# The rest of the third step with 64-column stationaries, a spectrum in two parts, and the two halves in another order

## The chip, the cores and the metric

The kernel runs on one core of a Trainium2 chip. The metric is the device time of one execution in microseconds: the median of three runs, and for the reading of stages one execution taken by the hardware profiler. The engines are named as in the profile: PE is the matrix engine (PEld its loading of stationary operands), DVE the vector engine, ACT the scalar engine, POOL GpSimd, SP the engine that here only issues transfers.

## The reference

A long convolution along 12480 positions for 128 channels, multiplied by its input, and then two feed-forward layers with a gate:

```python
h_filt = (np.maximum(pos_emb @ w1, 0.0) @ w2) * np.exp(-0.01 * pos)[:, None]
Uf = np.fft.rfft(x * v, n=2 * S, axis=1)
Hf = np.fft.rfft(h_filt, n=2 * S, axis=0)
x = x * np.fft.irfft(Uf * Hf[None], n=2 * S, axis=1)[:, :S, :]
h = x @ moe_w_in;  x = (h * np.clip(h + 3.0, 0.0, 6.0) / 6.0) @ moe_w_out
h = x @ moe2_w_in; x = np.where(h > 0.0, h, np.exp(np.minimum(h, 0.0)) - 1.0) @ moe2_w_out
```

S is 12480, the layers are 128 to 2048 to 128, all in float32.

## The kernel before

The transform has length 179 x 128 and is done as products with tables, in four steps, before the two layers.

**First step** (`first`, L352 to L367): 90 frequencies (NK) of each of 128 channels. `first_u` evacuates the signal on ACT into the spectrum `Au`, in two halves of 64 channels: half 0 in the tail of the big tile `qb`, half 1 in the tile `au`. An element of `Au` is (channel d, frequency k, real or imaginary r), 180 numbers to a channel.

**Second step** (`second`, L430): in octets of 8 frequencies, a product on PE (L425), two products on DVE with the filter's spectrum (L439), a sum on POOL back into `Au` (L444). The last of these are those of octet 11, halves 0 and 1.

**Third step** (`third`, L448 to L480): for each channel one product with the table `cs` over 128 partitions. The stationary operand is a slice of `Au`, the moving one 64 columns of `cs`. `third_main` takes the first 64 frequencies (KM) of one channel, real part into bank 0 and imaginary part into bank 1 of a two-bank tile `q`, each against two column sets of `cs` that go to the two halves of the output's partitions; a group has 8 channels. `third_rest` takes the last 32 frequencies (of which 26 are new, the other 6 are met by zeros in a later table), so its stationaries have 32 columns, and four products side by side fill the 128 partitions of the output. `third_out` copies the second bank to SBUF on ACT (L462) and writes difference and sum on DVE (L464) into `main` and `own`. The order is main of half 0, rest of halves 0 and 1, main of half 1. `own` is then copied with its partition halves exchanged into `other` by four transfers on SP (L525), 4 MB in all. Between the groups of main of half 1, SP issues the loads of `xT` (L533, into `au`, which that half frees) and of the third and fourth table `ti` (L507).

**Fourth step** (`fourth`, L541): 17 batches. In each, `ti` is the moving operand and `main`, `own`, `other` are the stationaries (L546), first the 128-partition products (`most`), then the 64-partition ones (`rest`), in turn the other way round. DVE multiplies the result into `xp`, which lies on `au` (L623, L626). Four tiles `ti` rotate (TB); a batch's table is loaded when the batch four before it is done. SP also loads the first pieces of the layers' weights.

**Weights:** the arrays of the layers arrive as 64-bit numbers and are turned into float32 by `weight_steps` (L214), 32 jobs of 256 columns: a load from the ACT or SP queue, two ACT operations (L230, L231), three DVE operations (L242 to L244), a POOL sum (L247) and a store (L225) from the ACT queue. Step k issues the load of job k+2, begins job k+1 on ACT and stores job k-1. The calls of `convert(rate)` are strewn over the second, third and fourth step; each adds its rate to a sum, and for each whole number one step is taken: 0.6, 0.3 and 0.9 for a call in the second, third and fourth step (RATE, L258). 34 steps and the last store are needed in all; `convert(1000)` behind the fourth step takes whatever is left.

**The two layers** (L615 on): units of 12 matrix products, PE-bound; all their loads of weights beyond three early pieces are issued on SP behind the fourth step.

All orders are written out by hand; each engine takes its instructions in program order. `bank` hands out PSUM: four two-bank tiles, tags px and py in turn, so that PE may be at most four groups ahead of DVE.

## Time and profile before

| what | us |
|---|---|
| median of three runs (lowest, highest) | 1391.97 (1388.36, 1392.3) |
| the profiled execution | 1385.58 |
| its span, first to last instruction | 1383.8 |
| third step in it, first to last product | 176.06 to 249.43 |
| fourth step, from there to the first product of the layers | 249.43 to 304.92 |

Times in the rows are counted from the span's start. A matrix product of float32 stands in the trace as two records of PE and two of PEld. In a list of groups, "busy, mean ns" is followed by the engine's idle time in front of them and what ended it; "issue" is time in which an engine waited for nothing that the profile shows. In the chain of waits each piece has its start, its length and what was done in it.

### The profile page before, as it was taken

Reading aid. Unit: us, or ns where it says so; the run is one execution under the profiler, and the core shown is the slowest. Engines: PE = TensorE matmul, PEld = TensorE weight load, DVE = VectorE, ACT = ScalarE, POOL = GpSimd, SP = SyncE. Lnnn points to the kernel's source line nnn. Section 1 sums busy time; section 2 is a strip of 40 time slices with the busy share of each in tenths; the row PEclk is TensorE's granted clock in tenths of the full one; section 3 lists DMA queues with packets and bytes.
Section 4 is the critical chain, followed back from the end, with each engine's and each line's share of the span. In section 5 each row is a group of like instructions: output and inputs, shape, how many; then the busy total and the mean of one; then the engine's idle time right before and its main releaser. Section 6 shows DMA issues by size and latency. Waiting matters only on the chain.

```text
span 1383.8 us, 23826 instructions
## 1 busy us (share of the span) xinstructions
PE 1339.5 (97%) x9696; PEld 1140.3 (82%) x9696; DVE 1133.9 (82%) x1196; ACT 987.9 (71%) x1163; POOL 390.9 (28%) x278
## 2 busy tenths in 40 slices
PE   9999976599999999999999999999999999999998
PEld 9999976487788888888888888888888888888898
DVE  6737764379998888888888888888888888889897
ACT  5655522139887778877878777877787777787876
POOL 1026620031522223223222222322322222222223
PEclk9999999799999999999999999999999999999999
DMA  8913225971000000000000000000000000000000
GB/s 271 273 57 115 75 71 130 324 236 59 0 8 8 1 8 8 8 8 1 8 8 8 8 1 9 8 8 8 1 8 9 8 0 9 8 9 8 9 1 19
DMA packets 32093, 62.90 MB, mean 45 GB/s; under 512 B 3786, under 2 KB 9200, under 8 KB 31728
## 3 DMA queue, kind: packets, MB, share of 16 engines
q1 hardware_dynamic: 24640, 52.40, 12.4%
q10 hardware_dynamic: 7344, 8.98, 2.0%
q8 instruction: 76, 1.25, 0.4%
q14 instruction: 33, 0.27, 0.1%
HBM read 46.59 MB, written 10.58 MB: 41 GB/s over the span
## 4 chain that ended last, share of the span: by engine, by line
PE 90%; issue 3%; DVE 3%; DMA 2%; ACT 1%; POOL 0%; SPq 0%; ACTq 0%; DVEq 0%; POOLq 0%
PE o L746 36%; PE h L702 36%; PE pa L356 4%; PE q L453 4%; PE z L425 3%; PE y L546 2%; PE h L415 1%; PE r L406 1%; PE pr L310 1%; DVE gs L736 1%; DMA w<-w_scratch 1%; DMA ti<-in_ti 1%; DVE g L723 1%; DMA cv<-in_mw 0%; DMA au<-in_xT 0%
## 5 line engine op out<-in xcount | busy, mean ns | idle before, releaser
L746 PE MATMUL o<-gs,w 128*128 128x512 f32 (+1 forms) x2400 | 570.8, 386 | 0.4 <-DVE gs L736 0.3
L746 PEld LDWEIGHTS o<-gs,w 128*128 128x128 f32 x2400 | 445.0, 188 | 92.3 <-DVE gs L736 0.8
L715 POOL TENSOR_SCALAR a<-a 128x1024 f32<-128x1024 f32 (+1 forms) x200 | 292.0, 1460 | 725.9 <-ACT a L714 721.5
L736 DVE TENSOR_TENSOR gs<-g,gs 128x1024 fp32r<-128x1024 f32 (+1 forms) x400 | 483.7, 1210 | 4.5 <-ACT gs L731 3.7
L731 ACT CAST gs<-g 128x1024 fp32r<-128x1024 f32 (+1 forms) x400 | 409.8, 1024 | 55.2 <-DVE g L723 53.6
L723 DVE SCALAR_TENSOR_TENSOR g<-a,h 128x1024 f32<-128x1024 f32 (+1 forms) x200 | 238.7, 1194 | 123.3 <-ACT a L712 123.2
L702 PE MATMUL h<-xs,w 128*128 128x512 f32 (+1 forms) x1200 | 302.9, 388 | 0.4 <-DVE g L723 0.4
L702 PE MATMUL h<-x,w 128*128 128x512 f32 (+1 forms) x1200 | 297.9, 384 | 0.2 <-ACT a L714 0.2
L714 ACT ACTIVATE a<-h 128x1024 f32<-128x1024 f32 (+1 forms) x200 | 201.3, 1006 | 93.8 <-PE h L702 92.6
L702 PEld LDWEIGHTS h<-xs,w 128*128 128x128 f32 x1200 | 223.0, 188 | 49.2 <-DVE g L723 1.4
L702 PEld LDWEIGHTS h<-x,w 128*128 128x128 f32 x1200 | 223.1, 188 | 43.8 <-issue 0.5
L712 ACT ACTIVATE a<-h,bounds 128x1024 f32<-128x1024 f32 (+1 forms) x200 | 219.1, 1096 | 52.6 <-PE h L702 52.4
L725 DVE SCALAR_TENSOR_TENSOR g<-a,h 128x1024 f32<-128x1024 f32 (+1 forms) x200 | 237.4, 1187 | 0.2 <-POOL a L715 0.2
L247 POOL TENSOR_TENSOR cv<-cv 128x256 int32<-128x256 int32 x32 | 23.4, 732 | 127.8 <-DVE cv L244 127.8
L546 PE MATMUL y<-ti,qb 128*64 128x97 f32 (+3 forms) x1040 | 41.0, 261 | 14.5 <-DMA ti<-in_ti 11.5
L546 PEld LDWEIGHTS y<-ti,qb 128*64 128x64 f32 (+1 forms) x1040 | 37.5, 145 | 17.9 <-issue 7.6
L230 ACT ACTIVATE cv<-cv 128x256 f32<-128x256 f32 x32 | 14.3, 448 | 47.9 <-POOL cv L247 28.1
L444 POOL TENSOR_TENSOR qb<-qb,bp 128x1024 f32<-128x1024 f32 (+1 forms) x12 | 26.9, 2242 | 73.4 <-PE h L415 71.1
L356 PE MATMUL pa<-tab,cv 98*64 98x180 f32 x512 | 44.0, 316 | 0.0
L453 PE MATMUL q<-cs,au 128*32 128x64 f32 (+1 forms) x1024 | 27.7, 234 | 14.2 <-issue 14.2
L464 DVE TENSOR_TENSOR qb<-q,au 128x512 f32<-128x512 f32 (+2 forms) x34 | 20.7, 647 | 25.1 <-ACT au L462 22.2
L356 PEld LDWEIGHTS pa<-tab,cv 98*64 98x64 f32 x512 | 37.7, 137 | 3.3
(68 smaller groups left out, 806.8 us busy)
## 6 DMA issues: line engine op xcount, KB each, us to landing
uv<-in_xc SPq DMA_DIRECT2D x32, 196.0 KB
out_T<-y SPq DMA_DIRECT2D x23, 256.0 KB
au<-in_xT SPq DMA_DIRECT2D x8, 720.0 KB
qb<-in_gm SPq DMA_DIRECT2D x22, 256.0 KB
ti<-in_ti SPq DMA_DIRECT2D x16, 294.0 KB
cv<-in_mw ACTq DMA_DIRECT2D x18, 256.0 KB
uv<-in_vc SPq DMA_DIRECT2D x22, 196.0 KB
w_scratch<-cv ACTq DMA_DIRECT2D x32, 128.0 KB
```

What stands on the lines that cost most here:

```text
L356: nc.tensor.matmul(pa[f * HN:(f + 1) * HN, j, :2 * NK], lhsT=src(j, f), rhs=table[:, f], start=True, stop=True)
L453: nc.tensor.matmul(q[p:p + width, r, j * HN:(j + 1) * HN], lhsT=stationary(j, p, r), rhs=csr[:, r, p // width % 2], start=True, stop=True,)
L546: nc.tensor.matmul(y[c * HD:(c + 1) * HD, b, off:off + w], lhsT=lhsT, rhs=rhs[:, H1 - w:], start=(b, c) in fresh, stop=done, skip_group_ch ...
L702: nc.tensor.matmul(h[:, j], lhsT=wslice(2 * m - 2, a, 2 * u + j), rhs=x[:, b], start=i == 0, stop=i == 2)
L712: nc.scalar.activation(a, h, AF.Relu, bias=three)
L714: nc.scalar.activation(a, h, AF.Exp)
L715: nc.gpsimd.tensor_scalar(a, a, 1.0, 0.0, op0=ALU.min, op1=ALU.max)
L723: nc.vector.scalar_tensor_tensor(g, a, 6.0, h, op0=ALU.min, op1=ALU.mult)
L725: nc.vector.scalar_tensor_tensor(g, a, -1.0, h, op0=ALU.add, op1=ALU.max)
L731: nc.scalar.copy(t[:, 0], g)
L736: nc.vector.tensor_tensor(out=t[:, 1], in0=g, in1=t[:, 0].bitcast(F32), op=ALU.subtract)
L746: nc.tensor.matmul(o[:, :WID[t]], lhsT=wslice(2 * m - 1, a, 2 * u + j), rhs=gs[:, b, j], start=u == 0 and j == 0 and i == 0, stop=u == NU ...
```

## The change

The spectrum is split: `AuM` holds the first 64 frequencies of each channel (130 numbers to a channel, two of them padding), `AuR` the other 26 (54 numbers to a channel, two of them zero). `first_u` evacuates with two ACT operations in the place of one.

The rest of the third step takes real and imaginary part of a channel's 26 frequencies as one stationary of 52 columns (64 are read, the other 12 are neighbours whose results nobody uses). One product goes against a new column set, `csx`, of 68 columns; another takes a copy with real and imaginary part exchanged, made by ACT (`turned`, two operations for a group of 7 channels of both halves) in two small tiles that POOL clears first. The two halves of the channels fill the two halves of the output. ACT copies the second bank as before; DVE combines with four operations (`scalar_tensor_tensor`, the sign from a column) into `own` and `stage`. `stage`, not `own`, is the source of the exchange, and a transfer moves 52 partitions of 8704 bytes.

The order is: main of half 1, its first 32 channels; the rest of both halves in ten groups; the exchange; main of half 1, the other 32 channels; main of half 0. `main` of half 0 lies on `stage` and on `AuR` of half 0. `xT` comes in 13 pieces: four issued between the groups of the rest, nine between the groups of main of half 0. Six tiles `ti` rotate, four of them in the place of `AuM` of half 0. The rates are 0.55, 0.25 and 0.75. `fourth` does the 64-partition products first in the even batches; they now have 52 partitions. The order of the channels is the natural one, so two host permutations go.

```diff
-KM, KR = 64, 32
+KM, KR = 64, NK - 64
+KW = 2 * KR
+NG = len(BATCHES)
...
+    MS, RS = 2 * (KM + 1), 2 * (KR + 1)
+    AM, AR = HD * MS, HD * RS
+    SL = 2 * NG * HD * 2
+    MQ = N2 * HD
+    MAIN1, STAGE = 2 * SL, 2 * SL + MQ
+    AR0 = STAGE + SL
+    AM0 = max(AR0 + AR + GUARD, STAGE + MQ)
...
-    RATE = (0.6, 0.3, 0.9)
+    RATE = (0.55, 0.25, 0.75)
...
-        nc.scalar.mul(to, pa[:, :, :2 * NK].rearrange(form, r=2), scale)
+        for z, a, b in to:
+            nc.scalar.mul(z, pa[:, :, 2 * a:2 * b].rearrange(form, r=2), scale)
...
+    def turned(e0, n):
+        sw = sws[e0 // ET % 2]
+        for hf in range(2):
+            nc.scalar.copy(
+                sw[:, hf * ET * KW:(hf * ET + n) * KW].rearrange("p (e k r) -> p e k r", e=n, r=2), AuR[hf][:, e0:e0 + n, :, ::-1]
+            )
+
+    def third_rest(e0, n):
+        sw = sws[e0 // ET % 2]
+        q = bank("q", [128, 2, 4 * N2])
+        for j in range(n):
+            for r in range(2):
+                for hf in range(2):
+                    z, at = (sw, (hf * ET + j) * KW) if r else (ends[hf], (e0 + j) * RS)
+                    nc.tensor.matmul(
+                        q[hf * HD:(hf + 1) * HD, r, j * EW:(j + 1) * EW], lhsT=z[:, at:at + HD], rhs=csx[:, r, hf],
+                        start=True, stop=True,
+                    )
+        qs = half(q, n * EW)
+        for x, to in enumerate((own, stage)):
+            first, second = (
+                z.rearrange("p (e x m) -> p x m e", e=n, x=2)[:, x] for z in (q[:, 0, :n * EW], qs)
+            )
+            for o, (a, b) in enumerate(((second, first), (first, second))):
+                nc.vector.scalar_tensor_tensor(
+                    to[:, o, :, e0:e0 + n], a, column[:, 2 - o:3 - o], b, op0=ALU.mult, op1=ALU.add,
+                )
...
+    ET = 7
+    TB, TW = 6, max(BLOCKS) * H1
...
+    xcuts = [*range(0, AW, XP), AW, S]
...
+    for sw in sws:
+        nc.gpsimd.memset(sw, 0.0)
+    turned(*rests[0])
+    for s0 in range(0, HD // 2, 8):
+        third_main(1, s0, 8)
         convert(RATE[1])
-    for hf in range(2):
-        for out in [third_rest(hf, e0, n) for e0, n in groups([8] * 4)]:
-            out()
-            convert(RATE[1])
-    for a, b in ((0, 8), (8, HN // 2)):
+    for i, (e0, n) in enumerate(rests):
+        if i + 1 < len(rests):
+            turned(*rests[i + 1])
+        third_rest(e0, n)
+        if i in (1, 3, 5, 7):
+            load_x()
+        convert(RATE[1])
+    for o in range(2):
         for p in range(2):
             nc.sync.dma_start(
-                other[p * HD:(p + 1) * HD, :, a:b].rearrange("p o g h e t -> p o (g h e t)"),
-                own[(1 - p) * HD:(2 - p) * HD, :, a:b].rearrange("p o g h e t -> p o (g h e t)"),
+                other[p * HD:p * HD + KW, o].rearrange("p m e -> p (m e)"),
+                stage[(1 - p) * HD:(1 - p) * HD + KW, o].rearrange("p m e -> p (m e)"),
             )
-    for s0, n in groups([8] * 7 + [4, 2, 2]):
-        third_main(1, s0, n)
-        if (s0 + n) % EX == 0:
-            a, b = xload.pop(0)
-            nc.sync.dma_start(xp[:, a:b], xT[:, a:b])
-        if s0 in (16, 32):
-            load_ti(s0 // 16 + 1)
+    for s0 in range(HD // 2, HD, 8):
+        third_main(1, s0, 8)
+        convert(RATE[1])
+    for s0, n in groups([8] * 7 + [4, 4]):
+        third_main(0, s0, n)
+        load_x()
+        if s0 in (32, 40):
+            load_ti(s0 // 8 - 2)
         convert(RATE[1] if s0 < 56 else 0)
+    for i in range(4, TB):
+        load_ti(i)
...
-        for k, part in enumerate((most, rest) if i % 2 == 0 else (rest, most)):
+        for k, part in enumerate((rest, most) if i % 2 == 0 else (most, rest)):
```

## Rows read from the trace of the kernel before

**Rows 1.** The page, part 1: busy time and instructions of each engine

```profile
PE 1339.5 (97%) x9696; PEld 1140.3 (82%) x9696; DVE 1133.9 (82%) x1196; ACT 987.9 (71%) x1163; POOL 390.9 (28%) x278
```

**Rows 2.** Busy by stretch: length, PE, PEld, DVE, ACT, POOL, PEclk, DMA, GB/s

```profile
0.00:80.00 80.00, 78.87 (x921) 73.33 (x922) 52.98 (x127) 47.65 (x109) 5.56 (x10) 1.00 0.81 243
...
176.06:193.77 17.71, 17.71 (x513) 17.64 (x513) 12.25 (x25) 6.27 (x13) 5.84 (x7) 0.87 0.33 102
193.77:224.27 30.50, 17.71 (x1070) 16.19 (x1068) 14.08 (x25) 7.28 (x15) 1.61 (x3) 1.00 0.12 35
224.27:249.43 25.16, 17.78 (x469) 17.57 (x469) 11.90 (x24) 6.03 (x13) 1.46 (x2) 0.80 0.98 222
249.43:304.92 55.49, 40.95 (x1049) 37.50 (x1045) 31.02 (x64) 12.04 (x30) 12.52 (x16) 0.88 0.86 291
...
276.00:296.00 20.00, 20.00 (x598) 18.74 (x596) 15.64 (x31) 4.71 (x12) 5.14 (x7) 0.99 0.77 223
```

**Rows 3.** The chain of waits from 80 to 345 us, in order of time

```profile
195.04 1.99 PE q L453 x128
197.03 1.89 issue
...
224.27 7.87 PE q L453 x251
232.14 1.99 issue
234.13 5.51 PE q L453 x124
239.65 5.39 issue
...
250.11 6.44 DMA cv<-in_mw
...
263.46 9.81 DMA ti<-in_ti
...
298.97 1.65 issue
```

**Rows 4.** Transfers of the whole run: a queue's packets, MB, share; issues, KB each

```profile
q8 instruction: 76, 1.25, 0.4%
...
ti<-in_ti SPq DMA_DIRECT2D x16, 294.0 KB
cv<-in_mw ACTq DMA_DIRECT2D x18, 256.0 KB
...
w_scratch<-cv ACTq DMA_DIRECT2D x32, 128.0 KB
...
qb<-qb SPq DMA_DIRECT2D x2, 1536.0 KB
...
qb<-qb SPq DMA_DIRECT2D x2, 512.0 KB
```

**Rows 5.** Groups by line and shape, 176 to 250 us

```profile
L462 ACT COPY au<-q 128x512 f32<-128x512 f32 x15 | 8.8, 587 | 36.0 <-PE q L453 32.6 <-DVE qb L464 3.4
...
L464 DVE TENSOR_TENSOR qb<-q,au 128x256 f32<-128x256 f32 x2 | 0.7, 414 | 0.0
```

**Rows 6.** Instructions in order of time, 158 to 200 us

```profile
179.78 0.59 ACT L462 COPY tab<-q 128x512 f32<-128x512 f32 x1 [2.85 <-PE q L453]
...
181.30 0.73 POOL L444 TENSOR_TENSOR au<-qb,bp 128x256 f32<-128x256 f32 x1
```

**Rows 7.** Instructions in order of time at the end of the fourth step

```profile
301.13 0.45 ACT L230 ACTIVATE cv<-cv 128x256 f32<-128x256 f32 x1 [1.71 <-DMA cv<-in_mw]
...
301.87 0.42 DVE L242 SCALAR_TENSOR_TENSOR cv<-cv,bounds 128x256 f32<-128x256 f32 x1
...
304.92 5.37 PEld L702 LDWEIGHTS h<-xs,w 128*128 128x128 f32 x24
...
305.55 0.62 ACT L662 CAST xs<-au 128x512 fp32r<-128x512 f32 x1 [0.90 <-POOL cv L247]
...
306.63 1.12 ACT L712 ACTIVATE a<-h,bounds 128x1024 f32<-128x1024 f32 x1 [0.45 <-PE h L702]
```

More of the change, by code (lines that the diff above doesn't have):

```diff
@@ L81, in tables @@
     cs = np.concatenate([c[:, :HN], end, inner, c[:, :1], inner, -end, -c[:, 1:HN]], axis=1)
+    passes = (c, np.concatenate([c[:, :1], inner, -end], axis=1))
+    sets = np.full((2, NG, 2), -1)
+    for g, banks in enumerate(BATCHES):
+        for b, ms in enumerate(banks):
+            sets[b, g, :len(ms)] = ms
+    extra = [
+        np.where(order.ravel() < 0, 0.0, z[:, order.ravel()]) for z in passes for order in (sets, sets[::-1])
+    ]
+    cs = np.concatenate([cs, *extra], axis=1)
     ends = (m == 0) | (m == HN)
@@ L87, in tables, with entries @@
     none = np.zeros_like(t[0, 0])
-    def entries(ms):
+    def entries(ms, place):
         pairs = []
         for m in ms:
-            if m == 0:
-                pairs += [(t[0, 0], none), (t[0, 1], none)]
-            elif m == HN:
-                pairs += [(none, t[m, 0]), (none, t[m, 1])]
+            if m in (0, HN):
+                pairs += [(t[m, i], none)[::1 - 2 * (place and m == HN)] for i in range(2)]
             else:
@@ L165, in tile_kernel, with parts, spectrum @@
     lds = lctx.enter_context(tc.tile_pool(name="lds", bufs=1))
-    uv = lds.tile([H1, 10 * VT], F32, name="uv")
-    Au = [z.rearrange("p (d k r) -> p d k r", r=2, k=NK) for z in (qb[:, 2 * QW - AW:], au[:, :AW])]
+    uv = lds.tile([H1, 8 * VT], F32, name="uv")
+    def parts(z, at, n, w):
+        return z[:, at:at + n].rearrange("p (d k r) -> p d k r", k=w + 1, r=2)[:, :, :w]
+    AuM = [parts(qb, AM0, AM, KM), parts(au, 0, AM, KM)]
+    AuR = [parts(qb, AR0, AR, KR), parts(au, AM, AR, KR)]
+    ends = [qb[:, AR0:AR0 + AR + GUARD], au[:, AM:AW]]
+    for z in ends:
+        nc.gpsimd.memset(z[:, :AR].rearrange("p (d x) -> p d x", x=RS)[:, :, KW:], 0.0)
+        nc.gpsimd.memset(z[:, AR:], 0.0)
+    def spectrum(hf, k0, n):
+        return (AuM[hf][:, :, k0:k0 + n] if k0 < KM else AuR[hf][:, :, k0 - KM:k0 - KM + n])
     Ar = qb[:, :RW].rearrange("p (x f) -> p x f", f=FO)
     Rk = qb[:, :RW].rearrange("p (k c) -> p k c", k=NK)
-    main = qb[:, :QW].rearrange("p (o g c h e t) -> p o g c h e t", o=2, c=2, h=2, e=KR, t=2)
-    own, other = (
-        qb[:, QW + i * N2 * HD:QW + (i + 1) * N2 * HD].rearrange("p (o g h e t) -> p o g h e t", o=2, h=2, e=KR, t=2)
-        for i in range(2)
+    main = [
+        qb[:, z:z + MQ].rearrange("p (o g e t) -> p o g e t", o=2, e=HD, t=2) for z in (STAGE, MAIN1)
+    ]
+    own, other, stage = (
+        qb[:, z:z + SL].rearrange("p (o m e) -> p o m e", o=2, e=HD) for z in (0, SL, STAGE)
     )
@@ L177, in tile_kernel @@
         z[:H1, i * VT:(i + 1) * VT].rearrange("p (d f i) -> p d f i", f=2, i=HN)
-        for z in (uv, cv) for i in range(z.shape[1] // VT)
+        for z in (uv, cv, qb[:, RW + RF + D:RW + RF + D + 2 * VT]) for i in range(z.shape[1] // VT)
     ]
@@ L181, in tile_kernel @@
     xts, vts, uts = uvs[:DEEP], uvs[DEEP:2 * DEEP], uvs[2 * DEEP:]
-    rest = qb[:, RW:2 * QW - AW]
+    rest = qb[:, RW:AR0]
     GN = 8
@@ L468, in third_out, with half @@
             )
-    def third_main(hf, s0, n):
-        third(
-            hf, n, lambda j, p, r: Au[hf][:, s0 + j, :KM, r], HD,
-            lambda o: main[:, o, :, s0 // KR, hf, s0 % KR:s0 % KR + n],
-        )()
-    def third_rest(hf, e0, n):
-        return third(
-            hf, n, lambda j, p, r: Au[hf][:, p // HD * KR + e0 + j, NK - KR:, r], KR,
-            lambda o: own[:, o, :, hf, e0:e0 + n],
-        )
+    def half(q, n):
+        qs = qss[thirds[0] % len(qss)][:, :n]
+        thirds[0] += 1
+        nc.scalar.copy(qs, q[:, 1, :n])
+        return qs
@@ L554, in fourth @@
             off, k, found = 0, 0, []
-            for m in ms:
+            for t, m in enumerate(ms):
                 for sg in (1, 0):
```

113 lines of the change are left out of this document (59 added, 54 removed).

## The prediction

> **What bounds the kernel now.** Start with the page's first part [rows 1]: PE is busy for 97% of the span. That is an average over a long, full stage (the two layers, from 304.92 us on) and the steps before it, which aren't full; so look next at busy time by stretch [rows 2]. The third step takes 73.4 us (17.71 + 30.50 + 25.16), the fourth 55.5 us with PE busy for only 40.95. Nothing in the change touches the steady work of the layers. What can be won lies in these 128.9 us, and PE's own pace says how much.
>
> The chain of waits gives that pace. Main runs at 7.87 us for 251 records, 31.4 ns each [rows 3]; main's 512 records of a half need 16.1 us. The fourth step runs at 598 records in 20 us, 33.4 ns each [rows 2], so its 1040 records need 34.8 us. Both halves' main and the fourth step are therefore 67 us, and the rest has 1024 records in 30.5 us less the 46 records of main that fall into that stretch (1.4 us): 29.1 us.
>
> Three losses show. First, in the rest PE does 128 records in 1.99 us and then stands still for 1.89 us with nothing that it waits for ("issue") [rows 3]; the last such pauses are 1.6 us. These pauses don't fall on the ends of groups: 46 records of the rest precede the first one, then 128 between each two. The instruction queue moved 1.25 MB in 76 packets, 16.4 KB each [rows 4]; PE and PEld have 19392 instructions [rows 1], 64 bytes each if nearly all of these bytes are theirs, so a packet holds 128 products with their loads. I read the pauses as PE waiting for its next packet, one each 3.6 to 3.9 us. Main uses a packet in 128 x 31.4 ns = 4.0 us and just escapes. Second, while the copies run (DMA share 0.98, 222 GB/s), the pauses come to main too, 1.99 and 5.39 us [rows 3]: 515 records take 1.4 + 25.16 = 26.6 us where 16.1 would do, 10.5 us lost. Third, the fourth step waits for tables `ti`, which SP queues behind the copies and `xT` (9.81 us in the chain) [rows 3]: 55.5 us against 34.8.
>
> **The change part by part.** *First and second step.* ACT evacuates each of 32 tiles with two operations in the place of one, under 0.6 us more on an engine that is busy for 47.65 of 80 us; PE has 78.87 [rows 2]. Hidden; uncovered it would be at most some 6 us (32 x 0.2, the fixed part of an operation). One weight step fewer is taken in the second step: between nothing and three DVE operations of 0.42 us [rows 7]; taken at nothing.
>
> *Main of half 1, first part:* 256 records at the opening pace of 17.71 us for 513 [rows 2]: 8.8 us. Behind it a wait is added: ACT's `turned` stands ahead of the first evacuation and needs POOL's last sum, at 181.30 + 0.73 = 182.0 [rows 6], and the clearing of its tile (744 numbers on POOL, at most 3 x 0.73 us by the 256-wide sum, at least the fixed tenths of a microsecond; near 1). With two copies of 364 numbers at less than 0.59 us [rows 5], the first evacuation starts near 184.2 and not at 179.78 [rows 6]. Queued behind it are ACT's evacuations, then DVE's sums, then PE from the fifth group on; PE's four tiles cover it until about 185 us, so the delay itself costs PE little, but ACT and DVE begin the rest four groups behind.
>
> *Rest:* 1024 records become 512, of 68 columns: 31.4 x 68/64 = 33.4 ns, 17.1 us, and a packet then lasts 4.3 us, longer than 3.9, so the pauses go. What is late next is DVE: four operations of 238 numbers, at most 0.414 each by the 256-wide row [rows 5], with a quarter of a weight step 1.9 us for a group, 17.8 us for 9.14 groups, and 4 groups of arrears. ACT has 0.56 + 2 x 0.5 + 0.2 = 1.8 us. Bounds for PE's part 17.1 and 24 (all arrears paid); I take 19, nearer to the floor since PE may run four groups ahead. Gain: 10.
>
> *Exchange:* 4 x 52 rows of 8704 bytes are 1.81 MB, against 4 MB (two of 1536 and two of 512 KB [rows 4]): 0.43 of the loss of 10.5, 4.5 us. At 222 GB/s the copies take 8.2 us. DVE's writes of main of half 0 wait for their end (`stage` lies under them); PE has eight groups' work between, so this is covered up to some 12 us. A rule of the Trainium skill, "DMA: Bandwidth & Descriptors", section "Why a DMA increments its semaphore by 16 and not by 1", speaks against the new shape: the number of DMA engines that share a transfer is the largest up to 16 that divides the slowest dimension, so 52 rows get 13 where 64 got 16. By it the copies would take 10.1 us (an estimate) and the sum would be about 1 us more; no row here shows a transfer of 52 rows.
>
> *Rest of main:* 768 records at 31.4 ns, 24.1 us, plus those 4.5 and what nine pieces of `xT` (4.3 MB, 14.6 us at 291 GB/s [rows 2]) do to the packets: nothing, as between 276 and 296 us, where DMA share is 0.77 and PE never stops [rows 2], or the same loss per microsecond as the copies, 6.1. I take 2.5, nearer to the first row, since `xT` comes like the tables from memory.
>
> The third step's sum: 8.8 + 19 + 24.1 + 4.5 + 2.5 = 58.9 us against 73.4, so 14.5 less; it ends at 235.
>
> *Fourth step:* four tables are there or on the way before main ends, two more queue right behind, and `xT` is ahead of its use. Demand: 13 tables of 294 KB, 12.75 weight steps of 256 + 128 KB [rows 4] and 0.8 MB of weights, 9.5 MB, 33 us at 291 GB/s. So PE's 34.8 us bind, plus one pause of 1.65 [rows 3]: 36.4, which is 19.1 less. Other order, 52 instead of 64 rows: the same 1040 records.
>
> *Start of the layers:* the rates give 13.2 + 6.25 + 12.75 = 32.2 steps where 34 are needed (before: 36.6). Steps 33 and 34 and the last store now stand between the fourth step and the layers, in the queues of DVE, ACT and POOL. The last load is issued near the fourth step's end and lands some 3 us later; ACT 0.9, DVE 1.2, POOL 0.7, and ACT's store waits for that. ACT's first evacuation of the layers came 1.7 us after PE's start, behind just such a wait for POOL [rows 7]; now about 5.5. PE has three tiles and stops: plus 3.8 us, bounds 1 (the load was early) and 6.5 (a load of 6.44 [rows 3]).
>
> Sum: -14.5 - 19.1 + 3.8 = -29.8 us; on the profiled execution's 1385.58 that is 1355.8. Its own time is 6.4 below the median of the three runs, and the forecast is made for a median: 1362.
>
> **The rivals.** *The pauses stay.* If PE stands still for a cause that goes with the array's work and not with packets, the rest gains nothing: before, 512 products in fours are 128 turns of 64 columns, now 256 in pairs are 128 turns of 68; 29.1 x 68/64 = 31 us, 12 more: 1374. Against it: the pauses keep step with 128 records and not with groups, and main, with the same tiles, has none. The Trainium skill, "Runtime: NRT & Kernel Launch", section "Instruction fetch mechanics", says that fetching is hidden behind the engine's issue; by that rule the cause would be another and this rival's 1374 holds; the trace, with 1.89 us for each 16.4 KB, speaks against the rule. Chance 0.12.
>
> *Transfers stay the bound.* From the first copy to the fourth step's end the kernel moved 25.16 x 222 + 55.49 x 291 = 21.7 MB; 2.4 of it goes, 2.1 of `xT` come earlier: 17.2 MB from 208 us on. At 291 GB/s that ends at 267, under my 271; at 230, as while the copies ran, at 283: 1374. For it: shares of 0.98 and 0.86 [rows 2]; against: much of the fourth step's share fell while PE waited for queue order. Chance 0.15.
>
> *No stalls at all:* neither `xT` nor the last steps cost anything, and DVE keeps up: 1352. Chance 0.17.
>
> *Slower: DVE's scattered writes.* The four operations write runs of 7 numbers 256 bytes apart and read PSUM at a stride of 68. If that broke their pace, the rest would take as long as DVE needs. The other gains are 10 us less than the sum, so it decides above 19 + 30 = 49 us for the rest, 1.25 us an operation, three times the 256-wide row; at 1.5 us, 58 us, 1401. For it: no row has this pattern; against: the sums of before write scattered too and have 414 ns [rows 5]. Chance 0.05.
>
> **How the numbers follow.** Forecast 0.51, rivals 0.12, 0.15, 0.17, 0.05. Terms at their ends: rest -1.9 / +5, `xT` -2.5 / +3.6, layers -2.8 / +2.7, fourth step -1.6 / +4; not all fall one way, so the likeliest case has 1353 to 1374, which also takes in three rivals' centres; their own spread makes it 1348 to 1379, and what lies outside is the slow case and the two rivals together. A difference of 0.3% (4 us) is about what a measurement of this kernel can tell from no change. Faster by more: 0.92; same: 0.03 (both rivals and a dear start); slower: 0.05.
>
> **What would show it.** Right: 512 records of the rest in 17 to 21 us without pauses; third step ending near 235, fourth near 271 without waits for `ti`; the first evacuation of the layers 4 to 6 us behind PE's start. Wrong: pauses of 1.6 us or more per 128 records; operations of the rest above 0.5 us; PE waiting for DVE throughout the rest; waits for `ti` or for a load of weights in the fourth step.

## The result and the profile after

The changed kernel has a median of 1355.3 us (four runs, 1353.46 to 1356.6) against 1390.16 us of the kernel before in the same set: a ratio of 0.9754, 95% interval 0.972 to 0.9788. The profiled execution took 1354.19 us, its span 1352.4 us against 1383.8.

Four stages, cut at the first product of the third step, the first of the fourth and the first of the layers, show where the 31.4 us of the span went (us; all kernels of this document, each from its profiled execution; ratios are against the kernel before, run beside it):

| kernel | third step begins | third | fourth | layers | median | ratio, 95% interval |
|---|---|---|---|---|---|---|
| before | 176.1 | 73.4 | 55.4 | 1078.9 | 1390.16 | |
| after | 169.8 | 66.4 | 39.1 | 1077.1 | 1355.3 | 0.9754 (0.972 to 0.9788) |
| a1_rates | 171.8 | 67.1 | 39.8 | 1069.9 | 1349.74 | 0.9722 (0.9705 to 0.974) |
| a2_order | 170.1 | 62.2 | 41.5 | 1077.1 | 1352.37 | 0.9734 (0.9713 to 0.9755) |
| a3_rows64 | 170.4 | 65.6 | 40.3 | 1077.6 | 1356.27 | 0.9768 (0.975 to 0.9786) |
| b1_pad | 169.9 | 72.9 | 57.3 | 1078.9 | 1381.6 | 0.9951 (0.9934 to 0.9968) |
| b3_shift | 175.8 | 74.0 | 56.6 | 1069.8 | 1378.91 | 0.9938 (0.9918 to 0.9958) |
| a5_imm | 169.9 | 65.5 | 40.5 | 1078.0 | 1352.73 | 0.9748 (0.9732 to 0.9764) |
| a4_noexchange | 170.4 | 62.7 | 39.0 | 1078.2 | 1351.8 | 0.9738 (0.9722 to 0.9754) |
| b2_groups4 | 175.5 | 80.6 | 57.3 | 1078.8 | 1394.07 (one run) | |
| a6_pairs | 170.9 | 58.3 | 39.9 | 1078.3 | 1351.12 | 0.9731 (0.9707 to 0.9755) |
| a7_pairs_rates | 171.3 | 63.7 | 41.2 | 1069.9 | 1348.45 | 0.9704 (0.9673 to 0.9736) |
| a8_cover | 170.9 | 61.8 | 39.6 | 1069.9 | 1343.12 | 0.9675 (0.9652 to 0.9699) |
| a9_xlate | 170.7 | 66.2 | 43.2 | 1078.3 | 1358.27 | 0.9777 (0.9749 to 0.9805) |

The kernel before had medians of 1387.84 to 1388.3 us in the sets of the other kernels and 1390.16 in that of the kernel after, so a difference of two medians from different sets can be some 2 us off; the ratios are free of that.

So before to after is -6.3 (the third step begins earlier), -7.0, -16.3 and -1.8. The forecast had 0, -14.5, -19.1 and +3.8. The sum is nearly the forecast's -29.8, but not one of its four parts is: that is what the rest of this text is about.

The page's first part for the kernel after, which answers to [rows 1]: 512 records of PE fewer (256 products), and PE's share is one point higher.

```profile
PE 1321.7 (98%) x9184; PEld 1135.0 (84%) x9184; DVE 1144.7 (85%) x1218; ACT 996.2 (74%) x1216; POOL 397.1 (29%) x284
```

Busy time by stretch of the kernel after (the columns are those of [rows 2]): main of half 1's first part; the rest; the rest of main; the fourth step; the start of the layers.

```profile
169.78:179.89 10.11, 10.11 (x263) 10.11 (x265) 3.98 (x9) 3.12 (x7) 5.79 (x7) 0.76 0.67 209
179.89:201.00 21.11, 17.72 (x512) 17.11 (x508) 18.85 (x36) 13.83 (x34) 1.47 (x2) 0.92 0.33 97
201.00:236.20 35.20, 25.59 (x779) 24.49 (x775) 24.77 (x51) 9.47 (x21) 2.94 (x4) 1.00 0.70 222
236.20:275.31 39.11, 36.99 (x1040) 34.04 (x1040) 29.17 (x56) 11.74 (x29) 11.52 (x14) 1.00 0.80 247
275.31:300.00 24.69, 17.54 (x69) 13.73 (x68) 20.40 (x29) 16.82 (x22) 4.50 (x6) 0.86 0.59 181
```

The rest's 512 records keep PE busy for 17.7 us and take 21.1. The 768 records of main behind it (11 neighbours count with them) keep it busy for 25.6 us and take 35.2: most of what the third step still loses lies here. The fourth step has 2.1 us without work where before it had 14.5 [rows 2].

The chain of waits of the kernel after, second and third step, in the columns of [rows 3] (L463 is the second step's product, L491 main's, L523 the rest's, L533 the rest's combination on DVE, L497 main's, L598 the exchange):

```profile
93.59 1.94 PE z L463 x16
...
179.89 1.28 PE q L523 x42
181.17 0.73 issue
181.90 4.00 PE q L523 x126
185.90 2.58 issue
188.48 3.43 PE q L523 x55
...
196.02 9.07 DVE qb L533 x16
...
206.22 2.92 DVE qb L533 x8
209.14 2.36 DVE qb L497 x4
...
212.17 0.41 SPq L598
212.58 0.05 issue
212.63 10.82 DMA qb<-qb
```

Two pauses of PE, 0.73 and 2.58 us, are left in the rest. Behind the second the clock falls: from 188.48 to 191.70 us the granted clock is 0.50, the lower of its two levels (1.2 GHz), and 57 records take 3.22 us, where at full clock 126 took 4.00. Then the chain goes over to DVE, which works off the rest until 209.14, eight microseconds after PE has left it, and then to the exchange. The waits of PE from 201.00 to 236.30 us of the same kernel (in total, times, longest) price each of these for the rest of main:

```profile
PE q L491 <- issue: 5.2, 3, 2.7
PE q L491 <- DVE qb L533: 3.0, 2, 1.8
PE q L491 <- DVE qb L497: 1.1, 1, 1.1
```

5.2 us are pauses, 3.0 DVE's arrears, and 1.1 the exchange, for which DVE waits before it writes `main` of half 0.

The groups of DVE in the third step of the kernel after, which answer to [rows 5]:

```profile
L533 DVE SCALAR_TENSOR_TENSOR qb<-au,column,q 128x238 f32<-128x238 f32 x12 | 7.9, 659 | 2.1 <-ACT au L506 2.1
...
L497 DVE TENSOR_TENSOR qb<-q,tab 128x512 f32<-128x512 f32 x12 | 7.7, 685 | 13.5 <-DMA qb<-qb 8.6 <-ACT tab L506 5.0
```

238 numbers take as long as main's 512.

Instructions in order of time where the fourth step of the kernel after ends and the layers begin, which answers to [rows 7] (L266 to L283 belong to a weight step, L777 is the layers' product, L787 its first evacuation):

```profile
275.31 1.65 PE L777 MATMUL h<-xs,w 128*128 128x512 f32 x6
...
281.26 0.43 ACT L266 ACTIVATE cv<-cv 128x256 f32<-128x256 f32 x1 [3.03 <-POOL cv L283]
...
283.08 0.72 POOL L283 TENSOR_TENSOR cv<-cv 128x256 int32<-128x256 int32 x1 [2.14 <-DVE cv L280]
...
284.72 2.11 ACT L787 ACTIVATE a<-h,bounds 128x1024 f32<-128x1024 f32 x2
...
287.14 4.69 PE L777 MATMUL h<-xs,w 128*128 128x512 f32 x12 [6.41 <-DVE g L798]
```

The leftover weight steps keep ACT from its first evacuation until 284.72, 9.4 us behind PE's start (before: 1.7 [rows 7]), and PE stands still for 6.41 us.

### The profile page after: what moved, and what is told of

Its sections match the earlier page's. It is cut to its first block, busy times and chain, and to the rows that moved or that the text cites. A ratio compares the mean times of both kernels' runs of the same rounds, so it can differ in the third digit from the quotient of the medians.

```text
span 1352.4 us, 22916 instructions
## 1 busy us (share of the span) xinstructions
PE 1321.7 (98%) x9184; PEld 1135.0 (84%) x9184; DVE 1144.7 (85%) x1218; ACT 996.2 (74%) x1216; POOL 397.1 (29%) x284
## 4 chain that ended last, share of the span: by engine, by line
PE 90%; DVE 4%; issue 2%; DMA 1%; POOL 1%; ACT 1%; SPq 0%; ACTq 0%; POOLq 0%; DVEq 0%
PE h L777 38%; PE o L821 38%; PE pa L392 4%; PE z L463 3%; PE y L623 3%; PE r L444 1%; PE h L453 1%; PE q L491 1%; DVE qb L533 1%; DMA qb<-qb 1%; DMA uv<-in_vc 1%; PE q L523 1%; DVE qb L497 0%; DVE cv L278 0%; POOL a L790 0%
## 5 line engine op out<-in xcount | busy, mean ns | idle before, releaser
L790 POOL TENSOR_SCALAR a<-a 128x1024 f32<-128x1024 f32 (+1 forms) x200 | 296.4, 1482 | 712.7 <-ACT a L789 712.7
L777 PE MATMUL h<-xs,w 128*128 128x512 f32 (+1 forms) x1200 | 300.2, 386 | 7.2 <-DVE g L798 6.4
L777 PE MATMUL h<-x,w 128*128 128x512 f32 (+1 forms) x1200 | 298.2, 384 | 0.2 <-ACT a L789 0.2
L777 PEld LDWEIGHTS h<-xs,w 128*128 128x128 f32 x1200 | 224.4, 189 | 52.9 <-DVE g L798 7.1
L777 PEld LDWEIGHTS h<-x,w 128*128 128x128 f32 x1200 | 223.2, 188 | 43.7 <-issue 0.5
L787 ACT ACTIVATE a<-h,bounds 128x1024 f32<-128x1024 f32 (+1 forms) x200 | 218.7, 1094 | 47.8 <-PE h L777 47.7
L283 POOL TENSOR_TENSOR cv<-cv 128x256 int32<-128x256 int32 x32 | 23.4, 731 | 108.6 <-DVE cv L280 104.8
L392 PE MATMUL pa<-tab,qb 98*64 98x180 f32 x512 | 42.7, 316 | 0.0
L392 PEld LDWEIGHTS pa<-tab,qb 98*64 98x64 f32 x512 | 39.1, 138 | 2.1
L266 ACT ACTIVATE cv<-cv 128x256 f32<-128x256 f32 x32 | 14.3, 446 | 33.3 <-POOL cv L283 14.7
L477 DVE TENSOR_TENSOR qb<-z,qb 128x1024 f32<-128x1024 f32 x12 | 14.7, 1225 | 25.0 <-ACT qb L456 15.3
L684 POOL TENSOR_TENSOR w<-w 128x512 fp32r<-128x512 f32 x12 | 17.1, 1434 | 39.2 <-ACT w L683 35.6
L753 ACT COPY y<-o 128x512 f32<-128x512 f32 (+1 forms) x25 | 14.5, 578 | 17.5 <-PE o L821 17.5
L482 POOL TENSOR_TENSOR au<-qb,au 128x1024 f32<-128x1024 f32 (+1 forms) x12 | 26.9, 2243 | 1.1 <-DVE au L477 1.1
```

What stands on the lines that cost most here:

```text
L392: nc.tensor.matmul(pa[f * HN:(f + 1) * HN, j, :2 * NK], lhsT=src(j, f), rhs=table[:, f], start=True, stop=True)
L482: nc.gpsimd.tensor_tensor(out=spectrum(hf, k0 + a, n), in0=m1, in1=m2[:, :, :, ::-1], op=ALU.add)
L777: nc.tensor.matmul(h[:, j], lhsT=wslice(2 * m - 2, a, 2 * u + j), rhs=x[:, b], start=i == 0, stop=i == 2)
L787: nc.scalar.activation(a, h, AF.Relu, bias=three)
L790: nc.gpsimd.tensor_scalar(a, a, 1.0, 0.0, op0=ALU.min, op1=ALU.max)
```

## The experiments

My theory after the result: the sum held because errors cancelled. The rest is held up by DVE's slow operations, the exchange by SP's issuing and by its bytes, the layers' start by the leftover steps; against this stand two gains that no step of the prediction has, in the second step and in the pace of the layers. The rival to each of these stands in the expectation of its run. Names with a change one thing in the kernel after, names with b in the kernel before.

### a1_rates: the old rates in the new kernel

```diff
-    RATE = (0.55, 0.25, 0.75)
+    RATE = (0.6, 0.3, 0.9)
```

> The kernel after, with the rates of before (0.6, 0.3, 0.9). Theory: the weight steps left over behind the fourth step hold ACT and DVE (PE waits 6.4 us for DVE before its third pair of products of the layers); with 37 steps asked for, the last is taken inside the fourth step. First ACT evacuation of the layers 2 us behind PE's start in the place of 9.4, time 5 to 8 us less than after, 1348. Rival (transfers bind the fourth step): the steps moved into it make it longer by as much, time within 2 us of after, and waits for ti or for in_mw grow in it.

The layers became 7.2 us shorter (1077.1 to 1069.9), the steps before them 3.4 us longer, as more weight steps lie there, so 3.8 us are gained in the profiled executions; the median is 5.6 us lower, by the two ratios 4.4 us (their intervals overlap by 0.002). The same place in the order of time of a1_rates:

```profile
278.74 5.56 PE L777 MATMUL h<-xs,w 128*128 128x512 f32 x23
...
280.43 1.12 ACT L787 ACTIVATE a<-h,bounds 128x1024 f32<-128x1024 f32 x1 [0.96 <-PE h L777]
```

The evacuation comes 1.7 us behind PE's start, as before. So the leftover steps are the cause, and the lower rates of the change cost more there than they gave before.

### a2_order and a5_imm: what makes DVE's operations slow

In the kernel after, these operations read single numbers, 68 apart in PSUM, and write runs of 7. a2_order exchanges the two loops, so that they read runs of 34 and write single numbers 256 bytes apart; a5_imm takes a constant in the place of the sign column, and so leaves out the alternating sign.

```diff
-                z.rearrange("p (e x m) -> p x m e", e=n, x=2)[:, x] for z in (q[:, 0, :n * EW], qs)
+                z.rearrange("p (e x m) -> p x e m", e=n, x=2)[:, x] for z in (q[:, 0, :n * EW], qs)
...
-                    to[:, o, :, e0:e0 + n], a, column[:, 2 - o:3 - o], b, op0=ALU.mult, op1=ALU.add,
+                    to[:, o, :, e0:e0 + n].rearrange("p m e -> p e m"), a, column[:, 2 - o:3 - o], b, op0=ALU.mult, op1=ALU.add,
```

> The kernel after, with the four DVE operations of the rest running over frequencies inside and channels outside: the two sources are read at a stride of one number and the result is written 256 bytes apart, before it was the other way round. Theory: the 657 ns of an operation of 238 numbers come from reading at a stride of 272 bytes; then near 400 ns, the rest 8 to 10 us shorter, the exchange begins that much earlier, time 6 to 9 us less than after, 1347. Rival 1 (the operation itself, a scalar from a column, costs it): still 657 ns and the same time. Rival 2 (strided access costs on either side): 650 to 700 ns, same time.

```diff
-                    to[:, o, :, e0:e0 + n], a, column[:, 2 - o:3 - o], b, op0=ALU.mult, op1=ALU.add,
+                    to[:, o, :, e0:e0 + n], a, 1.0, b, op0=ALU.mult, op1=ALU.add,
```

> The kernel after, with the sign of the four DVE operations of the rest as a constant of the instruction (1.0) and not a column of SBUF; the alternating sign is so left out. Theory: the column makes the 657 ns of an operation of 238 numbers; then 400 to 450 ns, the rest 8 us shorter, time 4 to 8 us less than after. Rival: the strided operands make it (618 ns when the strides were exchanged, so they don't make all of it): 620 to 657 ns and the same time.

The operation of 238 numbers in each kernel's list of groups, a2_order first:

```profile
L533 DVE SCALAR_TENSOR_TENSOR qb<-au,column,q 128x238 f32<-128x238 f32 x12 | 7.4, 618 | 1.5 <-ACT au L506 1.5
```

and a5_imm:

```profile
L533 DVE SCALAR_TENSOR_TENSOR qb<-q,au 128x238 f32<-128x238 f32 x12 | 7.1, 593 | 0.0
```

657 ns (a mean of 652 to 674 in the five kernels that leave this operation alone) fell to 618 with the loops exchanged and to some 595 without the column. Both theories had expected 400 to 450 ns. The column costs some 60 ns, and the operation stays slow with single numbers at a distance on either side. Neither run's interval parts its median from that of the kernel after, though a2_order's third step is 4.2 us shorter and PE's waits for L533 in it fall from 3.0 us to 0.2.

### a6_pairs: the rest's results in pairs

The product writes its results as pairs, the evacuation and the combination then read runs of 238 and write runs of 14.

```diff
-        qb[:, z:z + SL].rearrange("p (o m e) -> p o m e", o=2, e=HD) for z in (0, SL, STAGE)
+        qb[:, z:z + SL].rearrange("p (o g e t) -> p o g e t", o=2, e=HD, t=2) for z in (0, SL, STAGE)
...
-                        q[hf * HD:(hf + 1) * HD, r, j * EW:(j + 1) * EW], lhsT=..., rhs=csx[:, r, hf],
+                        q[hf * HD:(hf + 1) * HD, r, :n * EW].rearrange("p (m e t) -> p e m t", e=n, t=2)[:, j], lhsT=..., rhs=csx[:, r, hf].rearrange("p (m t) -> p m t", t=2),
...
-                    to[:, o, :, e0:e0 + n], a, column[:, 2 - o:3 - o], b, op0=ALU.mult, op1=ALU.add,
+                    to[:, o, :, e0:e0 + n].rearrange("p g e t -> p g (e t)"), a, column[:, 2 - o:3 - o], b, op0=ALU.mult, op1=ALU.add,
```

> The kernel after, with the rest's results laid in pairs of frequencies: PE writes q pair by pair, so that DVE's four operations read runs of 238 numbers and write runs of 14, and own keeps two frequencies of a channel side by side, as main does. Theory: operations that read or write single numbers at a distance take 1.7 to 1.9 ns a number, those in pairs 1.07 (a sum of 512 numbers 683 ns), and the column adds 60; so 414 + 60 = 470 ns in the place of 657, the rest 7 us shorter, then PE's pace or ACT's decides it, time 4 to 7 us less than after. Rival (the operation of this kind is slower in itself whatever the layout): above 590 ns, the same time.

The same group of a6_pairs:

```profile
L533 DVE SCALAR_TENSOR_TENSOR qb<-q,column,au 128x238 f32<-128x238 f32 x12 | 5.5, 457 | 0.0
```

457 ns, 200 less, with the column still there. So the layout costs 200 ns an operation, and the column's 60 come on top. On the last group, of 34 numbers, the column costs the same (272 ns in the kernel after, 209 in a5_imm) and the layout only 26 (246 in a6_pairs): the column is paid by the operation, the layout by the number. The third step is the shortest of all variants, 58.3 us. PE's list of waits no longer has L533 (3.0 us in the kernel after); its pauses are 4.3 us in the third step instead of 8.5, which the edit doesn't explain and which is counted neither for nor against it. The Trainium skill, "SBUF — State Buffer", section "Specifications (TRN2)", says that SBUF has lines of 16 bytes and needs at least two hits in a line for full bandwidth. The step from single numbers to runs agrees with it in kind; no run here shows the lines themselves, and one of the two operands that are read lies in PSUM, which no run parts from the other. The median, 4.2 us lower, isn't parted from that of the kernel after by the intervals; of the 8.1 us by which the profiled third step is shorter, 4.2 are such pauses.

### a3_rows64 and a4_noexchange: the exchange

```diff
-                other[p * HD:p * HD + KW, o].rearrange("p m e -> p (m e)"),
-                stage[(1 - p) * HD:(1 - p) * HD + KW, o].rearrange("p m e -> p (m e)"),
+                other[p * HD:(p + 1) * HD, o].rearrange("p m e -> p (m e)"),
+                stage[(1 - p) * HD:(2 - p) * HD, o].rearrange("p m e -> p (m e)"),
```

> The kernel after, but each transfer of the exchange moves 64 partitions and not 52 (2.23 MB in the place of 1.81). Theory by the skill's rule (52 rows go to 13 engines, 64 to 16): 10.8 us from issue to the release of DVE become 10.8 x 13/16 x 64/52 = 10.8, no change: the bytes grow as the engines do. Rival (16 engines already share 52 rows): 13.3 us, 2.5 us later, time up to 2.5 us more. Either way DVE's wait for the exchange (8.6 us) moves by as much.

The last transfer of the exchange in the chain of waits of a3_rows64:

```profile
211.08 11.63 DMA qb<-qb
```

64 rows are 64 / 52 = 1.23 times the bytes, so by bytes alone 10.82 us would become 13.3; 11.63 is nearer to no change, and the time as a whole doesn't tell the two kernels apart. The trace shows more than these two numbers. In the kernel after, the semaphore of each of the four transfers is raised once at its issue and 13 times as its data land; in a3_rows64 it is raised 16 times. The four transfers land at 216.04, 218.46, 220.92 and 223.45 us, 2.4 to 2.5 us apart, and the first three of a3_rows64 2.5 us apart with 23% more bytes (its last, 3.4 us behind the third, makes the difference). By the rule of the Trainium skill that the prediction weighed ("DMA: Bandwidth & Descriptors", section "Why a DMA increments its semaphore by 16 and not by 1"), 52 rows get 13 engines and 64 get 16. The trace agrees with it, 13 landings and 16. The estimate by this rule for the four copies, 10.1 us, was also right for their pace, four times 2.5 us, where mine was 8.2.

From the first issue at 209.00 to the last landing at 223.45 they took 14.45 us all the same, because the first landed only after 7.04 us. What it waited for is not shown; loads and stores of the weights moved meanwhile. SP's issuing, which my theory named, doesn't bind: the last transfer was issued at 212.63, before the first had landed, and landed as far behind the third as the others behind theirs. The 3.6 us between SP's first issue and its last lie on a queue that does nothing else meanwhile, and the profile puts 1.4 us of them down to a wait for a weight step on DVE (L279):

```profile
209.00 5.71 SPq L598 DMA_DIRECT2D qb<-qb  x4
```

(the view in order of time of SP, kernel after). a4_noexchange leaves the transfers out and reads `own` where `other` was read, so the fourth step works with the wrong half of these numbers:

```diff
-    for o in range(2):
-        for p in range(2):
-            nc.sync.dma_start(
-                other[p * HD:p * HD + KW, o].rearrange("p m e -> p (m e)"),
-                stage[(1 - p) * HD:(1 - p) * HD + KW, o].rearrange("p m e -> p (m e)"),
-            )
...
-                            put(b, c, off, w, (own if b == c else other)[rows, o, 2 * i + t], ti[rows, at + k], done)
+                            put(b, c, off, w, own[rows, o, 2 * i + t], ti[rows, at + k], done)
```

> The kernel after without the exchange: the four transfers are left out, and the fourth step takes own in the place of other. Theory: DVE's wait of 8.6 us before it writes main of half 0 goes, PE's pauses behind it too (2.7 + 1.1 + 1.0 + 1.5 us), the third step is 5 to 7 us shorter, time 6 to 8 us less than after: what the copies still cost. Rival (pauses of PE come from xT as well, and the wait is covered): 0 to 3 us.

The third step became 3.7 us shorter. PE's waits in its rest of main:

```profile
PE q L491 <- issue: 3.7, 2, 2.1
PE q L491 <- DVE qb L533: 2.9, 2, 1.7
```

The wait for L497 (1.1 us) is gone, one pause with it, and DVE's arrears are as they were. So the exchange costs 3.7 us by these two executions (2.6 of them in this list), less than the theory's 5 to 7, and the pauses in main come without it too; that `xT` and the tables bring them is likely and not shown. By the intervals the two medians aren't parted.

### b1_pad and b3_shift: the two gains that were not foreseen

b1_pad gives a channel of the kernel before two numbers more, 728 bytes for 720; b3_shift makes the tile `au` 272 numbers wider, which only puts the tiles below it (first pieces of the layers' weights and one of their input tiles among them) 1088 bytes lower.

```diff
-    AW = 2 * NK * HD
+    AW = 2 * (NK + 1) * HD
...
-    Au = [z.rearrange("p (d k r) -> p d k r", r=2, k=NK) for z in (qb[:, 2 * QW - AW:], au[:, :AW])]
+    Au = [z.rearrange("p (d k r) -> p d k r", r=2, k=NK + 1)[:, :, :NK] for z in (qb[:, 2 * QW - AW:], au[:, :AW])]
```

> The kernel before, with one frequency of padding to a channel of the spectrum: 728 bytes from channel to channel and not 720. Nothing else moves but the ends of the pieces of in_xT. Theory: the second step of after is quicker (1.94 and 2.14 us for a group of products with the spectrum, 2.13 and 2.33 before) because the moving operand's stride is no longer a multiple of 16 bytes; then these products take 1.94 and 2.14 us here too, the third step begins 4 to 5 us earlier, at 171 to 172, time 4 us less than before. Rival (the split itself, or the filter's tiles, which lie elsewhere): 2.13 and 2.33 us, 176, time as before. Also: if the layers' pace (439 records in 100 us before, 443 after) is a matter of the run and not of the kernel, it differs here.

```diff
-    au = ...tile([128, 2 * NK * HD + 8 * N2], F32, name="au")
+    au = ...tile([128, 2 * NK * HD + 8 * N2 + 272], F32, name="au")
```

> The kernel before, with the tile au 272 numbers wider, as wide as after; nothing uses them. Tiles that are allotted below au on that side (the first three pieces of weights and one x tile of the layers) lie 1088 bytes lower, as in after. Theory: the layers are quicker in after (3090 records of PE in 700 us, 3061 before) because of where these tiles lie; then 3090 records here and the layers' 1078.9 us fall to about 1070, time 8 to 9 us less than before, 1380. Rival: another tile's place (those that lie on qb's side), or something else that after changes: 3061 and 1079, time as before.

A group of the second step's products in the chain of waits of the kernel before:

```profile
95.03 2.13 PE z L425 x16
```

and of b1_pad:

```profile
94.28 1.83 PE z L425 x16
```

The third step of b1_pad begins at 169.9 us, as early as in the kernel after (169.8; before 176.1). So PE's pace in the second step goes with the distance at which it reads the moving operand (64 pairs of numbers, one from each channel): 720 bytes in the kernel before, 728 in b1_pad, 520 in the kernel after, where the same group took 1.94 us. In b3_shift, where `au` begins 1088 bytes lower and the distance is that of before, these groups keep their 2.13 us and the third step begins at 175.8; so another place alone doesn't do it. In the kernel after, 22.5 such groups at 0.19 us make 4.3 of the 6.3 us; the other 2 go with the lower rate of weight steps, by a1_rates, which has the old rate and begins its third step at 171.8.

PE in 700 us of the layers (length, busy, records, granted clock, DMA share, GB/s), kernel before:

```profile
400.00:1100.00 700.00, 700.00 (x3061) 1.00 0.02 7
```

and b3_shift, with the same line as the kernel after:

```profile
400.00:1100.00 700.00, 700.00 (x3090) 1.00 0.02 7
```

PE never idles in either, at the same clock, and yet gets through 29 records more, 0.9%. b3_shift shortens the layers by 9.1 us and nothing else. b1_pad, whose tiles below `au` lie 512 bytes lower, keeps 3061 records. So it hangs on where tiles lie, and the new layout happens to have the better place. The trace of the kernel before narrows it to the tiles that b3_shift moves. Where a product of the first layer (`h<-xs`) reads one of the three early pieces of weights or the early input tile `xs0`, or both, its records follow each other at 230.4 to 233.1 ns; where it reads neither, at 226.7, as all of the second layer's (`h<-x`) do. In b3_shift and in the kernel after all of them have 226.7. The records of `o<-gs` right behind a slow product are slow too, though their operands lie elsewhere; why, and which property of the address does it, stays open.

### b2_groups4: do the pauses go with groups

In the kernel before, the rest in 16 groups of 4 channels for 8 groups of 8. The combination of a group comes right behind its products, so `own` overwrites part of half 0's spectrum before later groups read it: those results differ, the number of products doesn't, and the first half has waits between DVE and PE that the kernel before hasn't.

```diff
-        for out in [third_rest(hf, e0, n) for e0, n in groups([8] * 4)]:
-            out()
-            convert(RATE[1])
+        for e0, n in groups([4] * 8):
+            third_rest(hf, e0, n)()
+            convert(RATE[1] / 2)
```

> The kernel before, with the rest of the third step in 16 groups of 4 channels in the place of 8 of 8; products and instructions of PE are the same, the groups end every 64 records. Theory (PE waits for its next packet of instructions): pauses still lie 128 records apart, 1.6 to 1.9 us long, the rest as long as before within 1 us. Rival (the pause belongs to a group's tile): pauses every 64 records, or gone.

The chain of waits of b2_groups4, second half of the rest:

```profile
213.44 1.99 PE q L453 x127
215.44 1.44 issue
216.88 1.99 PE q L453 x127
218.87 1.72 issue
```

The groups are 64 records now and the pauses are still 127 records apart. So they don't go with groups. That they are PE's wait for its next block of instructions, the traces show by their timing, though no run takes the fetching away. They hold each packet of the instruction queue (76 before, 72 after, 16.4 KB each): the pause of the kernel before that ends at 198.92 us [rows 3] ends 1.32 us behind the end of a packet at 197.60. So it is with all 12 of its pauses of over 0.2 us from the third step to the layers, 1.25 to 1.6 us behind a packet's end, with the 8 of the kernel after (1.25 to 1.57), and over all fourteen kernels with 125 of 126 (1.2 to 1.7). While the copies of the kernel before run, its packets begin 5.9 and 10.8 us apart, where they were 3.3 to 4.2 apart before, and there the pauses are 1.99 and 5.39 us long [rows 3]. The Trainium skill, "Runtime: NRT & Kernel Launch", section "Instruction fetch mechanics", says that the cost of crossing a block is mostly hidden. The trace disagrees: PE pauses up to 1.89 us for a block at a DMA share of 0.12 and 5.39 at 0.98 [rows 2].

### a7_pairs_rates, a8_cover and a9_xlate: put together, and the early pieces

a7_pairs_rates is a6_pairs with a1's rates. a8_cover moves 16 channels of main of half 1 from ahead of the rest to behind it, so that the exchange has 4 us more work of PE beside it, and two early pieces of `xT` from the rest to behind main:

```diff
-    for s0 in range(0, HD // 2, 8):
+    for s0 in range(0, HD // 4, 8):
...
-        if i in (1, 3, 5, 7):
+        if i in (1, 3):
...
-    for s0 in range(HD // 2, HD, 8):
+    for s0 in range(HD // 4, HD, 8):
```

> The kernel a6 with the rates of before, 0.6, 0.3, 0.9. Theory (the gains lie in different stages and add): 5.5 us less than a6, 1343 to 1347. Rival (the fourth step then waits for transfers, since it begins earlier): no more than 2 us less than a6.

> The kernel a7 with 16 and not 32 channels of main of half 1 ahead of the rest, and 48 behind the start of the exchange; two pieces of in_xT come early and not four. Theory: the exchange gets 4 us more of PE's work beside it, DVE's wait of 8.6 us falls to 4 or less and the third step gets 2 to 4 us shorter. Rival: PE's pauses for instructions during the transfers are what the time goes by, not DVE's wait; then within 1 us of a7, or up to 2 us more, since two pieces of in_xT come later.

a7_pairs_rates has 1348.45 us. The layers are as short as a1's. Its third step is 63.7 us and not a6's 58.3; PE's pauses in main account for it, 8.4 us against 2.8, with the same products and transfers. So their sum varies by some 5 us between kernels that hardly differ, and whether from run to run too, one profile of each can't say. a8_cover has 1343.12 us, 5.3 below a7, from which the intervals don't part it; its own (0.9652 to 0.9699) lies below that of the kernel after and of all single changes. In the third step of a8_cover neither PE nor DVE waits for the exchange; what PE still waits for there is this:

```profile
PE q L491 <- issue: 6.9, 4, 3.5
PE q L491 <- DVE bp L477: 1.9, 1, 1.9
PE q L523 <- ACT sw L512: 1.0, 2, 0.8
```

Pauses, and little else. The pauses in main, 6.9 us against a7's 8.4, are no part of what the edit was made for. They make most of the 1.9 us by which the third step is shorter, and in a7's third step too PE has no wait for L497, which waits for the exchange. So that a8_cover gains by covering the exchange is not shown.

a9_xlate takes the early pieces of `xT` out altogether:

```diff
-        if i in (1, 3, 5, 7):
-            load_x()
```

> The kernel after, but with no piece of in_xT issued in the rest: the first nine follow the exchange and the last four the tables 4 and 5. Theory (early loads are what freed the fourth step of its waits): 2.1 MB more in the stretch behind the exchange, 6 to 8 us of transfers; tables arrive later, waits for ti or xT come back in the fourth step, time 3 to 8 us more than after. Rival (six tables and fewer copied bytes are enough): within 2 us of after.

The fourth step grew by 4.1 us, the median by 3.0 (the intervals overlap). Not by waits for `xT` or `ti`, as I had expected; in PE's waits of the fourth step of a9_xlate

```profile
PE y L621 <- issue: 5.2, 4, 1.9
```

stands where the kernel after has

```profile
PE y L623 <- issue: 1.4, 3, 0.8
```

The transfers move 263 GB/s in this step where in the kernel after it is 247; that the denser traffic brings the pauses back is likely and not shown.

## Why the prediction was right and where it was not

The forecast of 1362 us was 6.7 above the median of 1355.3, and the sum of -29.8 us stands beside -31.4 in the profiled executions. Of the 6.7, only 1.6 are the sum's. The rest is the step from the profiled execution to the median, put at 6.4 from before, which was 1.1 for the kernel after. That the sum comes so near is luck: two gains that it doesn't have make up for savings that it put too high. Its steps, by what they measured:

- **Second step, "taken at nothing": -6.3.** Not a hidden cost but a gain that I didn't look for. The new spectrum has another distance between channels, and the pace of the products that read it depends on that (b1_pad); this is 4.3 us. The other 2 go with the weight step, which the prediction named and put at nothing (a1_rates, one execution). It named ACT's extra operation too, but not PE's own operand.
- **Main of half 1, first part, 8.8 us: 10.1.** At a granted clock of 0.76; the opening pace of before was read at 0.87 [rows 2]. The low clock cost 2.3 us there (0.13 x 17.71) and costs 2.4 here (0.24 x 10.11, both estimates), so it belongs to the stage's beginning and not to the records. By half of the records the forecast took half of it.
- **Rest, 19 us on PE: 21.1.** PE's own work came near the forecast (17.7 against 17.1), though for another reason: at full clock a record takes no longer than main's (4.00 us for 126, 31.7 ns, and not 33.4), and the 3.2 us at the lower clock behind a pause make up for it. The pauses didn't quite go: two, 3.3 us together. And the bound on DVE's operation was wrong: at most 0.414 us by the nearest row, 0.657 measured. That row writes and reads pairs; the new operation has single numbers on one side and a column, 200 and 60 ns (a6_pairs, a5_imm). The rival "slower: DVE's scattered writes" named this mechanism, at a size (1.25 us an operation) that it didn't reach. It cost 3.0 us of PE's waits, paid not in the rest but in main behind it. So two of the prediction's own signs of being wrong came here: operations above 0.5 us, and a pause above 1.6.
- **Rest of main, 24.1 + 4.5 + 2.5 = 31.1 us: 35.2.** Of the 4.1 us more, 3.0 are DVE's arrears and 1.5 PE's busy time (25.6 against 24.1, 11 neighbours in it); the loss to the transfers, 7.0 forecast, was 5.2 of pauses and 1.1 for the exchange. So that term came near, but the pauses in main differ by some 5 us between kernels that hardly differ, and the copies themselves took 14.45 us from the first issue and not 8.2: each lands in 13 parts, as the rule has it, and the first lands only after 7.04 us, for which the sum has no term.
- **Fourth step, 36.4 us: 39.1.** Right in mechanism: no wait for `ti` is left, PE binds. The pace was 37.0 us for 1040 records, 35.6 ns each, where 33.4 was read from a stretch of before. PE was no slower: 128-partition records follow each other at 42.3 ns and the others at 21.2 in both kernels. But that stretch held 320 of the quick ones in 598, and the whole step has half and half, which makes 0.8 of the 2.2 us (an estimate); the rest is open.
- **Start of the layers, +3.8 us: +7.3.** Right in mechanism, the evacuation 9.4 us behind PE's start and not 5.5; the size was above my upper bound of 6.5. a1_rates undoes it.
- **Pace of the layers, "nothing in the change touches" it: -9.1.** Wrong. It touches it by moving tiles (b3_shift).

The two unforeseen gains are 15.4 us; the shortfalls are 7.5 in the third step, 2.7 in the fourth and 3.5 at the layers. Without the gains the time would have been about 1370 us, inside the range too, but above the forecast and not below. Of the rivals, "the pauses stay" fell (512 records in 21.1 us and not 31), "transfers stay the bound" fell (no waits for tables), and "no stalls at all", 1352, is nearest in its number and wrong in its reason: there were stalls.

## What to carry to other kernels

A total that comes out right proves none of its terms: compare stage by stage, and give a term to each operand whose address or distance a change moves, even where the work stays the same. Read a pace from a stretch that has the mix of the whole stage. Price a new operation on DVE by a row with the same runs (single numbers, pairs, long runs) on both sides, not by a row of the same size. Work that a change takes out of a busy stage must be followed to where it is done instead; here it stood ahead of the first evacuation of the next stage and cost more there than it gave.

## What was not expected of the hardware

- PE's product with a moving operand of 64 pairs of float32 numbers, 720 bytes from pair to pair, takes 2.13 us for a group of 16 records, at 728 bytes 1.83 us (b1_pad, same kernel otherwise), at 520 bytes 1.94 us.
- PE's pauses without a wait end 1.2 to 1.7 us behind the end of a packet of instructions, 125 of 126 of them over all kernels.
- PE's steady pace in the layers, never idle and at full clock, differs by 0.9% (3061 and 3090 records in 700 us) when some tiles lie 1088 bytes lower. The first layer's records that read these tiles are slow (230.4 to 233.1 ns against 226.7); why is open.
- DVE's operation on 238 single numbers at a distance takes 618 to 657 ns, on the same numbers in runs 457, and a sign from a column costs some 60 ns more than a constant, for 34 numbers as for 238.
- A transfer of 52 rows within SBUF lands in 13 parts and one of 64 rows in 16, in nearly the same time (2.4 to 2.5 us apart and 2.5).
- Between the first and the last issue of four transfers within SBUF 3.6 us passed on SP; the four took it 5.6 to 6.2 us in all, in the kernel before and in each variant that has them.
